# Loading the first two weight units in pieces, and moving two preparation steps behind the first tanh

## The chip, the cores and the metric

The kernel runs on one core of a Trainium2 chip. The metric is device time in microseconds (us) for one execution, on that core. Engines are named as the profile names them: PE (matrix products; PEld are its weight loads), DVE (vector engine), ACT (scalar engine), POOL (GpSimd) and SP (which issues most DMAs). Each engine takes its instructions in a fixed order and waits at each for what it needs.

## What is computed

Attention with two kinds of masks over 8 batches, 8 heads, 576 tokens and 64 dimensions, and then a gated feed-forward layer on the 4608 resulting rows of 512 numbers:

```
scores = q @ k.T / 8            # heads 0-3: the 32 keys up to the query; heads 4-7: every 4th key of 128
attn   = softmax(where(mask, scores, -1e9))
x      = (attn @ v), heads side by side          # (4608, 512)
g, val = x @ w_gate, x @ w_val                   # (4608, 1536)
out    = (g * sigmoid(g) * val) @ w_out          # (4608, 512)
```

All inputs and outputs are float32. To keep that precision, the kernel splits each number into a high half in fp32r, which PE multiplies fast, and the rest, the low half; a product is made as high x high, low x high and high x low.

## The kernel before

**Stages.** The rows of x are worked on as columns, in three chunks of 512 columns and then three pairs of chunks with a faster product scheme. The first chunk is the one that matters here. Its attention (four packs, m = 0 to 3) and the preparation of the first weights run together in the first 30 us, in an order that is written out by hand. After that, one **step** s handles 128 of the 1536 hidden columns: PE makes the gate product `bg` (12 matmuls of 128x512), the value product `bv` (12) and, for step s-1, the output product `bo` (12). Step 0 is made in two passes in `gv_first` (L590), as the halves of x come; the others by `gv_mm` (L578) and `out_mm` (L630). In steps 1 and 2 the eight products that need a high half of the weights come first and the four with the low half last.

**What one step does besides.** ACT takes the tanh of `bg` (L608); DVE multiplies it with `bg` (`dve_u`, L613), which also frees the bank of `bg` for the next step, and then with `bv` (`dve_h`, L618); ACT casts the result to its high half (`h_hi`, L623) and POOL subtracts to get the low half (`h_lo`, L628).

**Weight units.** The weights come from memory as 24 units of 128 x 768 numbers, two for each step (units 2s and 2s+1), each as 768 pairs of 32-bit words of a 64-bit number. A unit goes through five stages, named by the letters of `STAGES = "ETBHL"`:

- E, `w_exp` on ACT (L253): scales the upper words,
- T, `w_shift`: shifts the lower or the upper words, on ACT (L270) for units 0, 1, 3, 5, 6, 8, 9, 11, 13, ... and on DVE (L273) for units 2, 4, 7, 10, 12,
- B, `w_bits` on DVE: joins the two words into one float32 (L280 after an ACT shift, L283 after a DVE one), called the **joining** below,
- H, `w_split_hi` on ACT (L290): the **cast** to the high half,
- L, `w_split_lo` on POOL (L294): the subtraction that gives the **low half**.

Stages E and T work in the loaded buffer; B writes one of three buffers (chosen by the unit's number modulo 3, for units up to 19), so stage T or B of unit u must wait until the low half of unit u-3 has been taken. The stages of units 0 and 1 are cut into parts by `SPLIT = {0: (0, 2, 3), 1: (0, 1, 3)}` in thirds of a unit: the first part of unit 0 is two thirds, that of unit 1 one third, and these are all that step 0 needs. The rest of unit 1 (two thirds) goes into the first output product, `bo` of step 0.

**Loads.** `w_load` (L230) issues the DMA of the next unit on SP into one of six buffers, once the buffer's earlier unit has been joined. All loads of the first part go through SP's queue in the order of the code at L674 to L693: queries, keys and values of the four packs, unit 0 ahead of the values of packs 2 and 3, then unit 1, the rest of the masks, units 2 to 5 and the data of pack 4. SP keeps at most eight DMAs outstanding.

**What sets the order.** The first attention and units 0 to 3 follow the string at L708, word by word: Q, S, X, T, K, A, N, U are steps of the attention, H and L after it the split of x, Y and Z idle matmuls, `W`n the next whole stage n (numbers into "ETBHL"), `V`nup part p of stage n of unit u. What comes after (the loop at L992) is put in order by a scheduler, which picks by its own estimate of when each instruction is ready, with some orders held by `behind`. So a stage taken from the string may end up in another place against others on the same engine than the code suggests.

**The fifth pack.** Pack 4 belongs to the second chunk. Its scores are made on PE in step 2, and its `results` (L522) after step 4 or 5; these need `far_keys` (L511), a transpose on DVE.

## Time and profile before

| | before |
|---|---|
| median of 3 runs | 892.26 us (892.11 to 893.58) |
| the profiled execution | 890.97 us |
| its span, first to last instruction | 889.2 us |
| PE busy | 879.5 us, 99% of the span |
| DVE, ACT, POOL busy | 76%, 43%, 31% of the span |
| DMA | 207.91 MB, 234 GB/s on average; 343 and 379 GB/s in the first two of 40 slices |
| granted TensorE clock | full in all 40 slices |

The profiled execution is 1.77 us longer than its span, and 1.29 us below the median. PE is busy nearly all the time, so the shares of the other engines say little on the whole; the time that PE does not work lies in the first 30 us, and there the other engines count.

### The profile page before, as it was taken

Reading aid. Unit: us, or ns where it says so; the run is one execution under the profiler, and the core shown is the slowest. Engines: PE = TensorE matmul, PEld = TensorE weight load, DVE = VectorE, ACT = ScalarE, POOL = GpSimd, SP = SyncE. Lnnn points to the kernel's source line nnn. Section 1 sums busy time; section 2 is a strip of 40 time slices with the busy share of each in tenths; the row PEclk is TensorE's granted clock in tenths of the full one; section 3 lists DMA queues with packets and bytes.
Section 4 is the critical chain, followed back from the end, with each engine's and each line's share of the span. In section 5 each row is a group of like instructions: output and inputs, shape, how many; then the busy total and the mean of one; then the engine's idle time right before and its main releaser. Section 6 shows DMA issues by size and latency. Waiting matters only on the chain.

```text
span 889.2 us, 19625 instructions
## 1 busy us (share of the span) xinstructions
PE 879.5 (99%) x7954; PEld 719.1 (81%) x7954; DVE 675.8 (76%) x1067; ACT 380.4 (43%) x615; POOL 272.3 (31%) x313
## 2 busy tenths in 40 slices
PE   8999999999999999999999999999999999999998
PEld 5778888888888888888888888888888888888886
DVE  7876658997899993777699966787799755556963
ACT  6877533433332342333355533343455423334451
POOL 4967631211121222323333112333322113333310
PEclk9999999999999999999999999999999999999999
DMA  9975518768778775887777877887766776666672
GB/s 343 379 287 203 165 59 296 258 224 273 240 267 277 251 247 199 260 242 239 247 234 235 261 249 252 259 251 240 231 217 217 244 224 190 189 192 195 196 221 97
DMA packets 78698, 207.91 MB, mean 234 GB/s; under 512 B 9456, under 2 KB 28016, under 8 KB 78608
## 3 DMA queue, kind: packets, MB, share of 16 engines
q0 software_dynamic: 27520, 100.16, 36.8%
q1 hardware_dynamic: 41872, 70.33, 22.6%
q10 hardware_dynamic: 9216, 36.17, 11.7%
q8 instruction: 63, 1.03, 0.5%
q14 instruction: 27, 0.22, 0.1%
HBM read 159.96 MB, written 42.47 MB: 228 GB/s over the span
## 4 chain that ended last, share of the span: by engine, by line
PE 96%; DMA 2%; DVE 1%; ACT 0%; issue 0%; DVEq 0%; SPq 0%
PE bo L934 33%; PE bv L934 12%; PE bg L934 12%; PE bo L636 11%; PE bg L587 11%; PE bv L587 11%; PE two L522 3%; PE two L459 2%; DMA at_float<-qkb 1%; DMA at_int<-w 1%; ACT at_int L253 0%; DVE at_int L283 0%; DVE at_int L280 0%; DVE at_int L273 0%; ACT at_int L270 0%
## 5 line engine op out<-in xcount | busy, mean ns | idle before, releaser
L934 PE MATMUL bo<-at_float32r 128*128 128x512 f32 x1296 | 306.1, 390 | 0.0
L934 PEld LDWEIGHTS bo<-at_float32r 128*128 128x128 f32 x1296 | 242.5, 188 | 50.9
L861 POOL DMA_DIRECT2D at_float32r<-pieces x189 | 101.3, 536 | 351.0 <-PE bo L934 210.8
L895 DVE TENSOR_TENSOR at_float<-bo,at_float 128x512 f32<-128x512 f32 (+1 forms) x169 | 112.4, 679 | 66.7 <-PE bo L934 33.4
L895 DVE TENSOR_TENSOR at_float32r<-at_float,at_float32r 128x512 fp32r<-128x512 f32 (+1 forms) x147 | 112.2, 792 | 26.1 <-ACT at_float32r L924 19.5
L934 PE MATMUL bv<-at_float32r 128*128 128x512 f32 x486 | 128.2, 390 | 0.0
L934 PE MATMUL bg<-at_float32r 128*128 128x512 f32 x486 | 128.2, 390 | 0.0
L934 PEld LDWEIGHTS bg<-at_float32r 128*128 128x128 f32 x486 | 91.1, 188 | 19.0
L934 PEld LDWEIGHTS bv<-at_float32r 128*128 128x128 f32 x486 | 90.9, 188 | 19.1
L628 POOL TENSOR_TENSOR at_float32r<-at_float,at_float32r 128x512 fp32r<-128x512 f32 x36 | 51.5, 1431 | 172.8 <-PE bo L636 87.6
L636 PE MATMUL bo<-at_float32r,at_float32r 128*128 128x512 f32 x432 | 104.4, 390 | 0.0
L587 PE MATMUL bg<-at_float32r,at_float32r 128*128 128x512 f32 x420 | 101.9, 391 | 0.8 <-DVE at_float L613 0.8
L924 ACT CAST at_float32r<-at_float 128x512 fp32r<-128x512 f32 x126 | 75.4, 620 | 63.5 <-PE bv L934 16.3
L587 PE MATMUL bv<-at_float32r,at_float32r 128*128 128x512 f32 x420 | 101.7, 391 | 0.0
L636 PEld LDWEIGHTS bo<-at_float32r,at_float32r 128*128 128x128 f32 x432 | 80.7, 188 | 17.0
L587 PEld LDWEIGHTS bg<-at_float32r,at_float32r 128*128 128x128 f32 x420 | 78.3, 188 | 17.8 <-DVE at_float L613 1.2
L587 PEld LDWEIGHTS bv<-at_float32r,at_float32r 128*128 128x128 f32 x420 | 78.4, 188 | 16.6
L960 ACT ACTIVATE at_float<-at_float 128x512 f32<-128x512 f32 x72 | 45.4, 631 | 94.2 <-DVE at_float L895 94.2
L939 ACT COPY at_float<-bg 128x512 f32<-128x512 f32 x63 | 36.9, 586 | 87.8 <-PE bg L934 87.5
L895 POOL TENSOR_TENSOR at_float<-at_float,at_float 128x512 f32<-128x512 f32 x36 | 51.6, 1434 | 23.2 <-DVE at_float L963 13.0
L962 DVE SCALAR_TENSOR_TENSOR at_float<-at_float,at_float 128x512 f32<-128x512 f32 x72 | 49.4, 686 | 10.7 <-ACT at_float L960 10.1
L294 POOL TENSOR_TENSOR at_float32r<-at_int,at_float32r 128x768 fp32r<-128x768 f32 (+2 forms) x26 | 47.1, 1823 | 20.5 <-ACT at_float32r L290 20.5
(84 smaller groups left out, 856.3 us busy)
## 6 DMA issues: line engine op xcount, KB each, us to landing
at_float32r<-pieces POOLq DMA_DIRECT2D x189, 512.0 KB, 4.4
pieces<-at_float32r SPq DMA_DIRECT2D x126, 256.0 KB, 3.2
at_int<-w SPq DMA_DIRECT2D x24, 768.0 KB, 6.7
at_float<-vb ACTq DMA_DIRECT2D x31, 520.0 KB, 5.1
at_float<-qkb ACTq DMA_DIRECT2D x16, 640.0 KB, 6.6
out<-at_float SPq DMA_DIRECT2D x35, 256.0 KB, 4.0
at_float<-qkb ACTq DMA_DIRECT2D x15, 576.0 KB, 6.4
at_float<-at_float SPq DMA_DIRECT2D x128, 32.0 KB, 3.4
```

What stands on the lines that cost most here:

```text
L294: nc.gpsimd.tensor_tensor(out=lo, in0=wst[u]["y"][:, a:b].bitcast(F32), in1=hi, op=ALU.subtract)
L522: nc.tensor.matmul(out=two[BQ * j:BQ * j + BQ, p, (D + 1) * x:(D + 1) * (x + 1)], lhsT=t[r, BQ * i:BQ * i + BQ], rhs=v[r, i, :], start=Tru ...
L587: last["g", which] = nc.tensor.matmul(out=bank.rearrange("p (n c) -> p n c", n=2), lhsT=wcol(f, o, low), rhs=x[l][j], start=n == 0, stop=n ...
L628: last["l"] = nc.gpsimd.tensor_tensor(out=hl, in0=hst[i][0], in1=hst[i][1], op=ALU.subtract)
L636: nc.tensor.matmul(out=bank_o[j][:, :CH], lhsT=wcol(f, 2 * DM + P * j, low), rhs=x, start=f == 0 and low == 0 and x is hh, stop=f == NF - ...
L861: nc.gpsimd.dma_start(out=taken[asked], in_=pieces[asked % NPIECE])
L895: x = engine.tensor_tensor(out=out, in0=a, in1=b, op=op)
L924: nc.scalar.copy(out=o[:, 0], in_=src)
L934: nc.tensor.matmul(out=bank, lhsT=w, rhs=x, start=first and n == 0 and t in FRESH, stop=last and n == len(ops) - 1, skip_group_check=True)
L939: nc.scalar.copy(out=kept[KEPT[t]][r], in_=banks[0][r][:, :CS])
L960: nc.scalar.activation(out=f, in_=g, func=AF.Tanh, scale=0.5)
L962: nc.vector.scalar_tensor_tensor(out=f, in0=f, scalar=1.0, in1=g, op0=ALU.add, op1=ALU.mult)
```

## The change

Units 0 and 1 are loaded in two DMAs each. `w_load` takes only the first part of the cut (two thirds of unit 0, one third of unit 1); `w_rest` loads the rest. The rest of unit 0 is issued behind the values of pack 3, and the rest of unit 1 behind units 2 and 3, ahead of the masks. In the string, the scaling and the shift of unit 1 are done for its first third alone; the cast and the low half of unit 2 (`W3 W4`) and the joining of unit 3 (the last `W2`) are taken out. They come in the loop after the first tanh and `dve_u`, together with the scaling and shift of the rest of unit 1.

```
-            last["w"] = nc.sync.dma_start(out=t, in_=w[u // 2, u % 2].bitcast(I32))
+            now = slice(0, 2 * UT * SPLIT[u][1] if u in SPLIT else 2 * WU)
+            last["w"] = nc.sync.dma_start(out=t[:, now], in_=w[u // 2, u % 2].bitcast(I32)[:, now])
...
+    def w_rest(u):
+
+        o = 2 * UT * SPLIT[u][1]
+        last["w"] = nc.sync.dma_start(out=at(raw_at[u], 2 * WU, I32)[:, o:], in_=w[u // 2, u % 2].bitcast(I32)[:, o:])
...
         first_v(3, (act, act), sp)
+        w_rest(0)
         w_load()
+        w_load()
+        w_load()
+        w_rest(1)
         nc.sync.dma_start(out=consts[:, near:], in_=masks[:, near:])
...
-        for what in ("... V001 V101 Z2 A3 N2 U2 W0 "
-                     "Z3 H2 L2 W1 N3 V201 V301 V401 U3 W0 H3 L3 V210 V310 V410 W0 W1 W2 W1 W3 W4 W2").split():
+        for what in ("... V001 V101 Z2 A3 N2 U2 V010 "
+                     "Z3 H2 L2 V110 W0 N3 V201 V301 V401 U3 H3 L3 V210 V310 V410 W0 W1 W2 W1").split():
...
-        w_upto(L=W + 3, H=W + 4 - (s == 0))
+        if s > 0:
+            w_upto(L=W + 3, H=W + 4)
...
             if s == 0:
                 w_upto(T=4, B=4, H=4)
+                w_part("E", 1, 1)
+                w_part("T", 1, 1)
                 dve_h(0)
```

What this does to the order of instructions shows on POOL first. There, behind the first chunk's x, stand the low halves of units 2 and 3 (`128x768`), the low half of the rest of unit 1 (`128x512`, L294) and `h_lo` of step 0 (L628). Buffers `at_776` hold joined units (numbers 345, 409, 427 stand for units 0, 1, 2 and every third unit after). Before:

```order
L294 TENSOR_TENSOR at_1536_float32r<-at_776_int_427,at_1536_float32r 128x768
L294 TENSOR_TENSOR at_1536_float32r<-at_776_int_345,at_1536_float32r 128x768
L294 TENSOR_TENSOR at_1536_float32r<-at_776_int_409,at_1536_float32r 128x512
L628 TENSOR_TENSOR at_512_float32r<-at_512_float_216,at_512_float32r 128x512
L294 TENSOR_TENSOR at_1536_float32r<-at_776_int_409,at_1536_float32r 128x768
```

And now (lines L300 and L634 are L294 and L628 of before; the buffers are 347, 411, 429):

```order
L300 TENSOR_TENSOR at_1536_float32r<-at_776_int_429,at_1536_float32r 128x768
L300 TENSOR_TENSOR at_1536_float32r<-at_776_int_347,at_1536_float32r 128x768
L634 TENSOR_TENSOR at_512_float32r<-at_512_float_218,at_512_float32r 128x512
L300 TENSOR_TENSOR at_1536_float32r<-at_776_int_411,at_1536_float32r 128x512
L300 TENSOR_TENSOR at_1536_float32r<-at_776_int_411,at_1536_float32r 128x768
```

`h_lo` of step 0 now stands ahead of the low half of unit 1's rest.

On DVE, from the joining of unit 3 to the second `dve_h`: `bg` marks `dve_u` (L613), `bv` marks `dve_h` (L618), `128x3x256` are whole units and `128x2x256` the rest of unit 1. Before:

```order
L280 SCALAR_TENSOR_TENSOR at_776_int_345<-at_1536_int_185 128x3x256
L613 SCALAR_TENSOR_TENSOR at_512_float_216<-at_512_float_216,bg 128x512
L280 SCALAR_TENSOR_TENSOR at_776_int_409<-at_1536_int_180 128x2x256
L618 SCALAR_TENSOR_TENSOR at_512_float_216<-at_512_float_216,bv 128x512
L273 TENSOR_SCALAR at_776_int_409<-at_1536_int_187 128x3x256
L283 SCALAR_TENSOR_TENSOR at_776_int_409<-at_1536_int_187,at_776_int_409 128x3x256
L280 SCALAR_TENSOR_TENSOR at_776_int_427<-at_1536_int_189 128x3x256
L613 SCALAR_TENSOR_TENSOR at_512_float_239<-at_512_float_239,bg 128x512
L618 SCALAR_TENSOR_TENSOR at_512_float_239<-at_512_float_239,bv 128x512
```

And now:

```order
L619 SCALAR_TENSOR_TENSOR at_512_float_218<-at_512_float_218,bg 128x512
L286 SCALAR_TENSOR_TENSOR at_776_int_347<-at_1536_int_185 128x3x256
L624 SCALAR_TENSOR_TENSOR at_512_float_218<-at_512_float_218,bv 128x512
L286 SCALAR_TENSOR_TENSOR at_776_int_411<-at_1536_int_181 128x2x256
L279 TENSOR_SCALAR at_776_int_411<-at_1536_int_189 128x3x256
L619 SCALAR_TENSOR_TENSOR at_512_float_241<-at_512_float_241,bg 128x512
L289 SCALAR_TENSOR_TENSOR at_776_int_411<-at_1536_int_189,at_776_int_411 128x3x256
L624 SCALAR_TENSOR_TENSOR at_512_float_241<-at_512_float_241,bv 128x512
L286 SCALAR_TENSOR_TENSOR at_776_int_429<-at_1536_int_191 128x3x256
```

The first `dve_u` stands ahead of the joining of unit 3, and the second `dve_u` and `dve_h` stand between the stages of units 4 and 5.

Further on, on DVE, from the fifth `dve_u` to the first instruction that needs pack 4's results (`two`); the transpose (L511) is `far_keys` of pack 4. Before:

```order
L613 SCALAR_TENSOR_TENSOR at_512_float_216<-at_512_float_216,bg 128x512
L273 TENSOR_SCALAR at_776_int_345<-at_1536_int_168 128x3x256
L511 STREAM_TRANSPOSE at_512_float_349<-at_512_float_318 128x512
L283 SCALAR_TENSOR_TENSOR at_776_int_345<-at_1536_int_168,at_776_int_345 128x3x256
L618 SCALAR_TENSOR_TENSOR at_512_float_216<-at_512_float_216,bv 128x512
L280 SCALAR_TENSOR_TENSOR at_776_int_409<-at_1536_int_180 128x3x256
L530 TENSOR_SCALAR at_8_float_317<-two 128x8
```

And now:

```order
L619 SCALAR_TENSOR_TENSOR at_512_float_218<-at_512_float_218,bg 128x512
L279 TENSOR_SCALAR at_776_int_347<-at_1536_int_168 128x3x256
L289 SCALAR_TENSOR_TENSOR at_776_int_347<-at_1536_int_168,at_776_int_347 128x3x256
L624 SCALAR_TENSOR_TENSOR at_512_float_218<-at_512_float_218,bv 128x512
L286 SCALAR_TENSOR_TENSOR at_776_int_411<-at_1536_int_181 128x3x256
L517 STREAM_TRANSPOSE at_512_float_351<-at_512_float_320 128x512
L536 TENSOR_SCALAR at_8_float_319<-two 128x8
```

`far_keys` stands behind the joinings of units 12 and 13. On PE, the results of pack 4 and the scores of pack 5 stood between `bv` of step 4 and `bo` of step 3; now they stand behind that `bo`. The two mask products of pack 4's scores stood in the middle of step 0's second pass and now stand behind it. On ACT the first tanh stands ahead of the cast of unit 2 instead of behind it, and the third to fifth tanh have more casts, scalings and shifts of units ahead of them. From step 6 on, the order on all engines is the same.

## Rows read from the trace of the kernel before

**Rows 1.** Busy time by stretch: length, PE, PEld, DVE, ACT, POOL, clock, DMA, GB/s.

```profile
20.00:30.00 10.00, 8.46 (x64) 5.72 (x64) 9.78 (x14) 9.42 (x16) 9.57 (x8) 1.00 1.02 413
30.00:60.00 30.00, 30.00 (x193) 24.60 (x192) 20.74 (x24) 24.58 (x35) 24.46 (x15) 1.00 0.88 318
```

**Rows 2.** PE's waits from 30 us to the end: total, times, longest.

```profile
PE bg L587 <- DVE at_float L613: 0.8, 1, 0.8
```

**Rows 3.** Timeline of PE: start us, us, engine, line, instruction, [idle before, releaser].

```profile
26.38 1.09 PE L596 MATMUL bg<-at_float32r,at_float32r 128*128 128x512 f32 x4
...
28.14 0.73 PE L596 MATMUL bv<-at_float32r,at_float32r 128*128 128x512 f32 x2 [0.21 <-POOL at_float32r L294]
29.62 3.02 PE L587 MATMUL bg<-at_float32r,at_float32r 128*128 128x512 f32 x12 [0.76 <-DVE at_float L613]
...
61.18 0.79 PE L522 MATMUL two<-at_float,at_float 64*32 64x65 f32 x60 [0.29 <-issue]
```

**Rows 4.** Chain that ended last, in time: start us, us, what.

```profile
35.36 2.72 PE bo L636 x12
38.08 2.72 PE bg L587 x12
...
55.45 2.72 PE bg L587 x12
...
62.65 2.95 PE bo L636 x12
65.60 2.72 PE bg L587 x12
```

**Rows 5.** Timeline of ACT.

```profile
21.45 0.92 ACT L253 ACTIVATE at_int<-at_int 128x768 f32<-128x768 f32 x1 [0.29 <-DMA at_int<-w]
...
27.52 0.83 ACT L290 CAST at_float32r<-at_int 128x768 fp32r<-128x768 f32 x1 [0.17 <-DVE at_int L283]
28.26 0.59 ACT L608 ACTIVATE at_float<-bg 128x512 f32<-128x512 f32 x1
...
43.17 0.84 ACT L290 CAST at_float32r<-at_int 128x768 fp32r<-128x768 f32 x1 [0.65 <-DVE at_int L283]
...
51.13 0.58 ACT L608 ACTIVATE at_float<-bg 128x512 f32<-128x512 f32 x1
```

**Rows 6.** Timeline of DVE.

```profile
27.43 1.47 DVE L280 SCALAR_TENSOR_TENSOR at_int<-at_int 128x768 int32<-128x768 int32 x1
28.88 0.69 DVE L613 SCALAR_TENSOR_TENSOR at_float<-at_float,bg 128x512 f32<-128x512 f32 x1
...
33.87 0.95 DVE L273 TENSOR_SCALAR at_int<-at_int 128x768 int32<-128x768 int32 x1 [2.21 <-POOL at_float32r L294]
...
39.28 1.87 DVE L280 SCALAR_TENSOR_TENSOR at_int<-at_int 128x768 int32<-128x768 int32 x1 [1.11 <-ACT at_int L270]
...
42.05 1.09 DVE L283 SCALAR_TENSOR_TENSOR at_int<-at_int,at_int 128x768 int32<-128x768 int32 x1
...
58.91 0.69 DVE L613 SCALAR_TENSOR_TENSOR at_float<-at_float,bg 128x512 f32<-128x512 f32 x1 [3.16 <-ACT at_float L608]
...
60.38 0.70 DVE L511 STREAM_TRANSPOSE at_float<-at_float 128x512 f32<-128x512 f32 x1
...
63.30 0.16 DVE L530 TENSOR_SCALAR at_float<-two 128x8 f32<-128x8 f32 x1
```

**Rows 7.** Line L280, the joinings after an ACT shift: duration ns min/median/max.

```profile
L280 DVE SCALAR_TENSOR_TENSOR at_int<-at_int x16: 458/950/1867, 18.5 to 108.9; 128x768 int32<-128x768 int32 x12, 128x512 int32<-128x512 int32 x2, 128x256 int32<-128x256 int32 x2
```

**Rows 8.** Timeline of POOL.

```profile
26.63 1.45 POOL L294 TENSOR_TENSOR at_float32r<-at_int,at_float32r 128x256 fp32r<-128x256 f32 x1
28.43 5.40 POOL L294 TENSOR_TENSOR at_float32r<-at_int,at_float32r 128x768 fp32r<-128x768 f32 x3 [0.35 <-ACT at_float32r L290]
33.80 1.29 POOL L628 TENSOR_TENSOR at_float32r<-at_float,at_float32r 128x512 fp32r<-128x512 f32 x1
36.86 3.47 POOL L294 TENSOR_TENSOR at_float32r<-at_int,at_float32r 128x768 fp32r<-128x768 f32 x2 [1.77 <-ACT at_float32r L290]
```

More of the change, by code (lines that the diff above doesn't have):

```diff
@@ L707, in attention_moe @@
     with tc.manual_schedule(engines={et.PE, et.DVE, et.Activation, et.Pool}):
-        for what in ("Q0 S0 Q1 Y2 S1 X0 Q2 X1 T0 S2 T1 K0 K1 Q3 X2 A0 T2 K2 S3 X3 N0 A1 V000 U0 T3 V100 K3 N1 A2 V200 U1 H0 L0 V300 V400 H1 L1 V001 V101 Z2 A3 N2 U2 W0 "
-                     "Z3 H2 L2 W1 N3 V201 V301 V401 U3 W0 H3 L3 V210 V310 V410 W0 W1 W2 W1 W3 W4 W2").split():
+        for what in ("Q0 S0 Q1 Y2 S1 X0 Q2 X1 T0 S2 T1 K0 K1 Q3 X2 A0 T2 K2 S3 X3 N0 A1 V000 U0 T3 V100 K3 N1 A2 V200 U1 H0 L0 V300 V400 H1 L1 V001 V101 Z2 A3 N2 U2 V010 "
+                     "Z3 H2 L2 V110 W0 N3 V201 V301 V401 U3 H3 L3 V210 V310 V410 W0 W1 W2 W1").split():
             first[what[0]](*[int(c) for c in what[1:]])
```

## The prediction

> **What bounds the kernel now.** The busy shares come first and say where not to look: PE works 99% of the span. PE's waits from 30 us to the end are then one wait of 0.8 us for `dve_u` [rows 2], and in the timeline a gap of 0.29 us ahead of pack 4's results [rows 3]; behind these PE has no slack anywhere. Two things follow. A microsecond that PE starts step 1 earlier can only be kept if nothing else makes PE wait later, and a microsecond of new waiting in the first steps stays until the end. The chain that ended last shows the same: from step 1 on it is PE's groups end to end, a dozen products in 2.72 us, that is 0.227 us each [rows 4]. Then the stretches. From 20 to 30 us ACT, DVE and POOL are busy 9.4 to 9.8 of 10 us; from 30 to 60 us they are busy 20.7 to 24.6 of 30 us, with the clock at full speed throughout [rows 1]. So between the start and the first output rows the three helpers have some 5 to 9 us of slack, and the question is at which instructions it lies.
>
> At the start, PE's first pass over `bg` ends at 26.38 + 1.09 = 27.47 [rows 3], but the first tanh starts at 28.26, behind the cast of unit 2 [rows 5]; `dve_u` then starts at 28.88, with the joining of unit 3 ahead of it until 28.90 [rows 6], and PE starts step 1 at 29.62 [rows 3]. That is the wait of 0.8 us.
>
> **The loads.** Between 20 and 30 us 413 GB/s arrive [rows 1]. Unit 1 was scaled from 21.45 on, after ACT had waited 0.29 us for it [rows 5], so it had landed by 21.43. A third of a unit is 256 KB, or 0.63 us at that rate. By my count of what now stands ahead of each load (an estimate from that rate), unit 2 has landed by 22.1, the rest of unit 1 by 25.2, and unit 4 near 27.5 as before. The rest of unit 1 is first touched by ACT behind the cast of unit 2, near 28.9, so 3.7 us of other work hide it. What the pieces give is the 0.29 us of waiting and two thirds of two ACT instructions of 0.92 us, 1.2 us, ahead of the first tanh [rows 5]; but the first tanh waits for PE's pass anyway, so I put this at nothing, at best 0.3 us.
>
> **The start of step 1: a gain.** With the cast moved behind it the first tanh runs at 27.5 to 28.1 (0.59), `dve_u` at 28.13 to 28.82 (0.69) [rows 5, 6]. PE's own pass still ends with the pair at 28.14 + 0.73 = 28.87 [rows 3], and the two mask products, now behind it (half of 0.227 us each), end with it or 0.1 us later. Step 1 starts at 28.95 in place of 29.62: **-0.65 us**.
>
> **POOL: the gain is lost.** The cast of unit 2 now runs at 28.05 to 28.9, so POOL starts on its low half at 28.95 where it did at 28.43. Before, three subtractions (units 2, 3 and the rest of unit 1) took 5.40 us, to 33.83, and `h_lo` came fourth, 1.29 us [rows 8]. Now `h_lo` comes third, and the rest of unit 1 ends at 28.95 + 5.40 + 1.29 = 35.64. Bounds: without any hold-up two units take 3.47 us [rows 8] and the two of 512 columns 1.29 us each, 35.0 in all; with one hold-up more, 36.2. I take 35.64, because the joinings of unit 3 and of the rest of unit 1 still fall beside these subtractions, as they did within the 5.40.
>
> What such a hold-up is, the rows show: a joining begun beside a subtraction takes 1.47 or 1.87 us in place of 0.95 [rows 6, 7], and both ended 0.82 us after the subtraction did (28.90 against 26.63 + 1.45 = 28.08, and 41.15 against 36.86 + 3.47 = 40.33) [rows 6, 8]. A joining that starts second waits for the end of the subtraction, and the reverse gives POOL its 5.40 for 4.76 of work.
>
> The Trainium skill ("SBUF — State Buffer", section "SBUF: two separate sides") has this as an exclusive lock: of a DVE instruction with two SBUF inputs and a GpSimd one, whichever starts first keeps the port for its whole length. By that rule alone, with DVE first at each meeting, POOL would end at the later bound, and the sum would be that of the heavier rival below; with POOL first it would end near 35.0. The 0.82 us agree with it; who comes first in the new order no run shows yet.
>
> Who waits for the 35.64? First PE. Step 1's `bg` takes 3.02 us and `bv` 2.72 [rows 3, 4], so the first output product runs at 34.69 to 34.92; the second needs the low half of unit 1's rest and waits 0.7 us. `bo` ends at 38.15 in place of 38.08: the 0.65 us are gone. Second, DVE: the shift of unit 4 uses that unit's buffer. Before, it waited 2.21 us for the same subtraction and started at 33.87 [rows 6]; now it starts at 35.65. Queued behind it on DVE are `dve_u` of step 1, the joining of unit 4, `dve_h` and the joining of unit 5, 1.8 us later than before, and PE's step 2 needs both `dve_u` and unit 4.
>
> **Step 2: a new wait of PE.** The shift ends at 36.6 (0.95), `dve_u` at 37.25 (0.69), the joining at 38.2 (0.95), the cast at 39.05 (0.84) [rows 5 to 7]. The `bg` of step 2 starts at 39.1 and not at 38.08, and takes 3.02 us, as the one behind a wait did, and not 2.72: +1.3 us. Its last four products need the low half of unit 4, which POOL has at 39.1 + 1.74 = 40.84 (half of 3.47) or, held up by the joining of unit 5, up to 0.95 later, while PE is there at 41.2: 0 to 0.6, I take 0.3. Sum from here: **+1.6 us**; the `bg` of step 4 starts at 55.45 + 1.6 = 57.05.
>
> **The units behind it, and pack 4.** `dve_h` of step 1 ends at 38.85, the joining of unit 5 at 39.8, its cast at 40.65. On ACT now come `h_hi` (as the tanh, 0.59), the scaling and the shift of unit 6 (0.92 each); each starts some 0.1 us before the end of the one ahead (28.26 against 27.52 + 0.83 = 28.35) [rows 5], so the shift ends at 42.9 and the joining of unit 6 starts at 42.95, where it was 39.28 [rows 6]: +3.7 us, twice what PE lost. From there to the end of the joining of unit 7 were 39.28 to 43.14, 3.86 us [rows 6], and now a `dve_u` (0.69) stands between: 47.5. From the cast of unit 7 to the end of the fourth tanh ACT took 43.17 to 51.71, 8.54 us, for ten other instructions [rows 5]; they are the same in another order, so that tanh ends at 56.0. It does not stop PE: `dve_u` ends at 56.75, 0.3 us before step 4 wants it. But behind it on DVE are a shift, `dve_h` and the joinings of units 10 and 11 (four of 0.68 to 0.95, the last beside a subtraction): unit 11 is joined at 61.1, cast by ACT at 62.0, and the fifth tanh, behind that cast now, ends at 62.6. Then DVE has the same six instructions as before from `dve_u` on, 58.91 to 63.30, 4.39 us [rows 6], with `far_keys` last and not third. They end at 67.0; with two joinings of six beside subtractions (0 to 0.9 each) I take 67.3.
>
> PE comes to pack 4's results after `bv` of step 4 and `bo` of step 3, 57.05 + 8.16 = 65.2, and stands there 2.1 us, where before it stood 0.29 for a transpose that ended at 61.08 [rows 3, 6]. Results and scores take 61.18 to 62.65, 1.47 us [rows 3, 4], and the group behind them 0.23 us more than 2.72 (2.95) [rows 4]. The `bg` of step 5 starts at 67.35 + 1.47 + 0.23 = 69.05 in place of 65.60 [rows 4]: **+3.45 us**. From step 6 on the orders are equal, and PE has nothing in which to make it up [rows 2].
>
> The profiled execution was 890.97 us, its span 1.77 us less; 890.97 + 3.45 = 894.4. The median of the runs is 1.29 us above the profiled one: 895.7.
>
> **Rivals.** *Heavier:* the joinings win the race against the subtractions, and on the way from the low half of unit 1's rest to `far_keys` four meetings (units 5, 7, 11 and 12) cost 0.4 us more each, half of the 0.82 that a meeting costs the later one. +1.6: 897.3. For it: the 5.40 for 4.76, three subtractions that lost 0.6 already. Against it: my sum has two of them in.
>
> *On the other side, not slower:* the slack of the helpers takes up the delay of 3.7 us before pack 4 asks for it. For it: 5 to 9 us of slack from 30 to 60 us [rows 1]. Its point: `far_keys` done by 65.2. Then PE has the wait of step 2 alone, +1.6: 893.9, or 893.0 where POOL has no hold-up and step 2 starts at 38.4. Against it: ACT's order is fixed, and what is idle in it stands ahead of casts that now come later still.
>
> *The change does what it says and nothing else:* the rest of unit 1 is in time, PE keeps its 0.65: 891.6. It needs the low half by 34.9, before POOL's lower bound, so it has little for it. That the pieces do not land as planned would show as a wait for a load; with 3.7 us of margin I give that nothing.
>
> **How the numbers follow.** About 0.2%, 1.8 us, is what a measurement of this kernel can tell from no change: slower begins at 894.04, faster below 890.48. My forecast, about 895.7 with 894.5 to 896.5 by its own bounds, has 0.66; the heavier case 0.17; the slack case 0.14; the kept gain 0.03. So slower 0.82, the same 0.16 and faster 0.02. The range goes from 893.4, in the middle of the slack case, to 898.0, the heavier one with 36.2 for POOL's bound.
>
> **What would show it.** Right: the first tanh near 27.5 and step 1 near 28.95; the rest of unit 1 subtracted by 35.6 on POOL, with PE waiting within the first `bo`; a wait of about 1 us at the second `bg` for a cast; the joining of unit 6 near 43; PE waiting about 2 us ahead of pack 4's results for the transpose, which ends near 67. Wrong: no wait at the results (then +1.6 at most), or waits of PE in steps 6 and later, which would mean that the delay of the units outlives pack 4 and the loss is larger.

## The result and the profile after

| | before | after |
|---|---|---|
| median, 6 runs each | 892.39 us (892.11 to 894.59) | 898.64 us (898.32 to 899.86) |
| the profiled execution | 890.97 us | 898.32 us |
| its span | 889.2 us | 896.2 us |

The change makes the kernel slower: the medians differ by 6.25 us, and the ratio estimated from all runs is 1.0066, with a 95% interval of 1.0053 to 1.0079. The forecast was +3.4 us, 895.7 us, with a range up to 898.0: the direction was right and the size too small. Lines from L246 on have moved by six in the changed kernel (L587 is now L593, L613 L619, L290 L296, L294 L300, L511 L517, L522 L528).

PE's waits from 30 us to the end, where before had one [rows 2]; columns are total, times, longest:

```profile
PE two L528 <- DVE at_float L517: 2.2, 1, 2.2
PE bg L593 <- DVE at_float L619: 0.6, 1, 0.6
PE bg L593 <- ACT at_float32r L296: 0.5, 1, 0.5
PE bo L642 <- POOL at_float32r L300: 0.4, 1, 0.4
PE bg L593 <- POOL at_float32r L300: 0.3, 1, 0.3
```

The wait of 0.8 us for the first `dve_u` is gone, and five others have come. Their places are in the timeline of PE, to be read against [rows 3, 4]:

```profile
25.86 1.23 PE L602 MATMUL bg<-at_float32r,at_float32r 128*128 128x512 f32 x4
...
28.59 2.06 PE L593 MATMUL bg<-at_float32r,at_float32r 128*128 128x512 f32 x8
30.99 1.21 PE L593 MATMUL bg<-at_float32r,at_float32r 128*128 128x512 f32 x4 [0.34 <-POOL at_float32r L300]
...
35.56 2.83 PE L642 MATMUL bo<-at_float32r,at_float32r 128*128 128x512 f32 x11 [0.38 <-POOL at_float32r L300]
38.87 3.42 PE L593 MATMUL bg<-at_float32r,at_float32r 128*128 128x512 f32 x12 [0.48 <-ACT at_float32r L296]
...
57.54 3.03 PE L593 MATMUL bg<-at_float32r,at_float32r 128*128 128x512 f32 x12 [0.60 <-DVE at_float L619]
...
68.23 0.81 PE L528 MATMUL two<-at_float,at_float 64*32 64x65 f32 x60 [2.21 <-DVE at_float L517]
...
69.73 4.49 PE L593 MATMUL bg<-at_float32r,at_float32r 128*128 128x512 f32 x12
```

Step 1 starts at 28.59. POOL's low half holds PE in `bg` of step 1 and in `bo` of step 0, a cast holds step 2, `dve_u` holds step 4, and the results of pack 4 wait 2.21 us for `far_keys`. The last line is the surprise: the `bg` of step 5 takes 4.49 us. In this view a dozen products take 2.88 us behind another group, 3.02 or 3.03 behind a wait or the small products, and 3.42 at step 2. The 3.42 hold a second wait, which shows at the weight loads: those of the last four products wait for the low half of unit 4.

```profile
41.08 0.77 PEld L593 LDWEIGHTS bg<-at_float32r,at_float32r 128*128 128x128 f32 x4 [0.54 <-POOL at_float32r L300]
```

The stretches around step 5 (length, PE, PEld, DVE, ACT, POOL, granted clock, DMA share, GB/s) say why its `bg` is slow:

```profile
66.00:69.80 3.80, 1.59 (x130) 1.41 (x129) 2.17 (x4) 2.19 (x3) 2.77 (x2) 0.96 0.67 210
69.80:74.20 4.40, 4.40 (x14) 3.51 (x14) 3.66 (x7) 0.00 (x0) 2.27 (x2) 0.65 0.92 363
74.20:77.00 2.80, 2.80 (x14) 2.30 (x13) 2.08 (x3) 2.75 (x5) 0.00 (x0) 1.00 0.36 149
```

Behind the wait the granted clock is 0.65 on average for 4.4 us, then full again; from 70 to 72 us it is 0.50, that is 1.2 GHz, half of the upper level of 2.4. In time at the lower level that is 4.4 x 0.35 / 0.5 = 3.1 us, and 3.8 x 0.04 / 0.5 = 0.3 us ahead of it: 3.4 us, which cost half of that, 1.7.

**Counted from one point.** The attention ahead of step 0 ends at another time in every execution: the first pass over `bg` ended between 26.86 and 28.03 us in the fifteen traces of the experiments. (It ended at 27.35 on average in the fourteen traces with loads in pieces, and at 27.78 in the three without, that of before among them. That may be the gain of the pieces that the forecast put at nothing; three traces are too few to show it.) So the starts of the later groups are best counted from there (27.47 before, 25.86 + 1.23 = 27.09 after), by the timeline's starts in both:

| start of `bg` of step | before | after | later by | as forecast |
|---|---|---|---|---|
| 1 | 2.15 | 1.50 | -0.65 | -0.65 |
| 2 | 10.45 | 11.78 | 1.33 | 1.2 |
| 3 | 19.49 | 21.39 | 1.90 | 1.6 |
| 4 | 27.82 | 30.45 | 2.63 | 1.6 |
| 5 | 37.97 | 42.64 | 4.67 | 3.45 |
| 6 | 46.13 | 52.41 | 6.28 | 3.45 |
| 7 | 55.92 | 62.25 | 6.33 | 3.45 |

The forecast read its starts from the chain [rows 4], where a group starts when the one before it ends. In the timeline a group that follows without a wait starts 0.16 us earlier (37.92 and not 38.08), so for step 2, which waits, the last column has 39.1 - 37.92.

The 6.33 us of the traces agree with the 6.25 of the medians. From there on both kernels do the same. The stretch from the `bg` of step 8 to the end took 797.3 to 798.7 us in all traces but that of e15 (804.0), without relation to the edits, so that nothing is read from differences under 1 us in a single trace's span.

POOL and DVE at the start of step 1, to be read against [rows 6, 8]. POOL:

```profile
28.52 4.58 POOL L300 TENSOR_TENSOR at_float32r<-at_int,at_float32r 128x768 fp32r<-128x768 f32 x2 [0.80 <-ACT at_float32r L296]
33.06 1.29 POOL L634 TENSOR_TENSOR at_float32r<-at_float,at_float32r 128x512 fp32r<-128x512 f32 x1
34.31 1.19 POOL L300 TENSOR_TENSOR at_float32r<-at_int,at_float32r 128x512 fp32r<-128x512 f32 x1
...
51.92 1.75 POOL L300 TENSOR_TENSOR at_float32r<-at_int,at_float32r 128x768 fp32r<-128x768 f32 x1
...
61.80 3.47 POOL L300 TENSOR_TENSOR at_float32r<-at_int,at_float32r 128x768 fp32r<-128x768 f32 x2
```

DVE:

```profile
28.36 0.95 DVE L286 SCALAR_TENSOR_TENSOR at_int<-at_int 128x768 int32<-128x768 int32 x1
...
35.54 0.95 DVE L279 TENSOR_SCALAR at_int<-at_int 128x768 int32<-128x768 int32 x1 [4.05 <-POOL at_float32r L300]
...
42.44 1.13 DVE L286 SCALAR_TENSOR_TENSOR at_int<-at_int 128x768 int32<-128x768 int32 x1 [3.02 <-ACT at_int L276]
...
52.15 2.07 DVE L486 TENSOR_TENSOR at_float<-at_float,at_float 128x512 f32<-128x512 f32 x1
...
63.66 2.42 DVE L289 SCALAR_TENSOR_TENSOR at_int<-at_int,at_int 128x768 int32<-128x768 int32 x1
...
67.47 0.70 DVE L517 STREAM_TRANSPOSE at_float<-at_float 128x512 f32<-128x512 f32 x1
```

The low half of unit 1's rest ends at 35.50, which is 8.41 us after the first pass (35.64 and 8.17 were forecast). The shift of unit 4 starts at 35.54 after 4.05 us of idle time, the joining of unit 6 at 42.44, and `far_keys` ends at 68.17. On ACT:

```profile
47.29 0.83 ACT L296 CAST at_float32r<-at_int 128x768 fp32r<-128x768 f32 x1 [2.82 <-DVE at_int L289]
...
54.25 0.63 ACT L498 ACTIVATE at_float<-at_float 128x512 f32<-128x512 f32 x1 [0.89 <-DVE at_float L486]
...
54.92 0.63 ACT L493 ACTIVATE at_float<-at_float 128x512 f32<-128x512 f32 x1
...
56.18 0.59 ACT L614 ACTIVATE at_float<-bg 128x512 f32<-128x512 f32 x1
```

From the cast of unit 7 to the end of the fourth tanh it is 47.29 to 56.77, 9.48 us. L498 and L493 are the two exponentials of pack 4.

### The profile page after: what moved, and what is told of

Read it like the earlier page. It is cut to its first block, busy times and chain, and to the rows that moved or that the text cites. A ratio compares the mean times of both kernels' runs of the same rounds, so it can differ in the third digit from the quotient of the medians.

```text
span 896.2 us, 19629 instructions
## 1 busy us (share of the span) xinstructions
PE 883.7 (99%) x7954; PEld 719.8 (80%) x7954; DVE 676.7 (76%) x1067; ACT 380.4 (42%) x617; POOL 272.8 (30%) x313
## 3 DMA queue, kind: packets, MB, share of 16 engines
q8 instruction: 63, 1.03, 0.5%
## 4 chain that ended last, share of the span: by engine, by line
PE 92%; DVE 1%; DMA 1%; ACT 0%; issue 0%; DVEq 0%
PE bo L944 33%; PE bv L944 12%; PE bg L944 12%; PE bo L642 10%; PE bg L593 10%; PE bv L593 10%; PE two L528 3%; PE two L465 2%; DMA at_int<-w 1%; DVE at_int L286 0%; DVE at_float L486 0%; ACT at_int L259 0%; ACT at_int L276 0%; DVE at_float L485 0%; DVE at_float L624 0%
## 5 line engine op out<-in xcount | busy, mean ns | idle before, releaser
L593 PE MATMUL bg<-at_float32r,at_float32r 128*128 128x512 f32 x420 | 104.4, 397 | 1.5 <-DVE at_float L619 0.6
L634 POOL TENSOR_TENSOR at_float32r<-at_float,at_float32r 128x512 fp32r<-128x512 f32 x36 | 52.3, 1453 | 174.6 <-PE bo L642 94.2
L593 PE MATMUL bv<-at_float32r,at_float32r 128*128 128x512 f32 x420 | 102.0, 392 | 0.0
L593 PEld LDWEIGHTS bg<-at_float32r,at_float32r 128*128 128x128 f32 x420 | 79.0, 190 | 20.4 <-POOL at_float32r L300 1.3
L593 PEld LDWEIGHTS bv<-at_float32r,at_float32r 128*128 128x128 f32 x420 | 78.4, 188 | 16.9
L300 POOL TENSOR_TENSOR at_float32r<-at_int,at_float32r 128x768 fp32r<-128x768 f32 (+2 forms) x26 | 46.6, 1802 | 26.1 <-ACT at_float32r L296 26.1
```

The costliest lines, as they stand in the source:

```text
L300: nc.gpsimd.tensor_tensor(out=lo, in0=wst[u]["y"][:, a:b].bitcast(F32), in1=hi, op=ALU.subtract)
L593: last["g", which] = nc.tensor.matmul(out=bank.rearrange("p (n c) -> p n c", n=2), lhsT=wcol(f, o, low), rhs=x[l][j], start=n == 0, stop=n ...
L634: last["l"] = nc.gpsimd.tensor_tensor(out=hl, in0=hst[i][0], in1=hst[i][1], op=ALU.subtract)
```

## The experiments

Every time is given against the kernel before, measured beside it on the same chip (on the chips used, its median was 891.35 to 892.45 us). The edits are against the changed kernel unless a line says otherwise, and e1 to e15 are numbered in the order in which they ran. The absolute times in the expectations are on the scale of the first measurement (892.39 before, 898.64 changed), so they are compared by their distance from the kernel before.

### Is it the clock, or something else at step 5

Two kernels give PE idle products in the place of the wait at the results. In both, a trace line tells more than the time does.

```diff
-        visits(m, a, a + 4)
+        visits(m, a + (m == 5), a + 4)
...
+        if s == 4:
+            with behind("o"):          # the last product of bo
+                idle(10, bank_g)
         attend(3 * s + 2)              # now holds pack 4's results
```

**e1, idle.** Expected:

> The changed kernel with ten idle products (bf16, 512 columns, into the bank of bg, which is free there) between bo of step 3 and pack 4's results, so that PE works through the 2.21 us in which it waited for far_keys; all other orders are unchanged. Theory A: the changed kernel's loss is 4.20 us of waiting up to the bg of step 5 and 1.70 us more because the clock was granted at 1.2 GHz behind that wait; with PE at work the results still start near 68.2, but the bg of step 5 takes 2.7 to 3.0 us in place of 4.42, and the time falls by 1.4 to 1.7 us, to about 897.1. Rival B: that group is slow for another reason (363 GB/s of DMA in this stretch, or the small products ahead of it), it stays at about 4.4 us, and the time stays at 898.6.

Measured: 897.34 us, 5.99 us above before (ratio 1.0065, interval 1.005 to 1.008), where the changed kernel was 6.25 above. PE's timeline:

```profile
66.03 2.33 PE L673 MATMUL bg<-at_float 128*128 128x512 bf16 x10
...
69.78 3.02 PE L593 MATMUL bg<-at_float32r,at_float32r 128*128 128x512 f32 x12
...
85.02 0.50 PE L642 MATMUL bo<-at_float32r,at_float32r 128*128 128x512 f32 x1
86.75 2.77 PE L642 MATMUL bo<-at_float32r,at_float32r 128*128 128x512 f32 x11 [1.23 <-issue]
```

With PE at work the group takes 3.02 us and not 4.49, at the same start of 69.8: the rival that something else slows it falls. The time, though, fell by 0.26 us only, where theory A said 1.4 to 1.7: 1.23 us are lost again within `bo` of step 5, with no releaser that the profile names. Counted from the first pass, the `bg` of step 6 starts 1.59 us earlier than in the changed kernel, and that of step 7 only 0.15.

```diff
+                for _ in range(2):
+                    nc.tensor.matmul(out=bank_g[:64]..., lhsT=ones, rhs=ones...)   # float32, 512 columns
+                idle(2, bank_g)
```

**e5, idle wide.** Expected:

> As the run with ten idle products, but with four that take as long (two in float32, four passes each, and two in bf16), so that PE's stream grows by six instructions and not by twenty. In the run before, bg of step 5 took 2.95 us at full clock, and then PE stood 1.23 us ahead of the second product of bo of step 5, with no engine named as releaser. Theory A: that new stall belongs to the longer stream of PE instructions; here it is gone or smaller, and the time is 4.5 to 4.9 us above the kernel before. Rival B: it belongs to the preparation, which is not ready earlier than in the changed kernel, whatever PE does in between; it stays at 1.2 us, and the time is 6.0 us above the kernel before.

Measured: 896.91 us, 5.47 us above before (1.0067, 1.005 to 1.0084).

```profile
85.75 1.43 PE L642 MATMUL bo<-at_float32r,at_float32r 128*128 128x512 f32 x5
87.52 1.89 PE L642 MATMUL bo<-at_float32r,at_float32r 128*128 128x512 f32 x7 [0.34 <-issue]
```

The new stall is 0.34 us and stands behind the fifth product instead of the first. The page counts 20 more PE and PEld instructions than in the changed kernel in the first of these and 12 in the second: eight fewer, four products with their weight loads, which is by how much the stall has moved. So it sits at one instruction of PE's stream, and it ends 1.73 and 1.77 us after PE has started the first product behind the small ones of pack 5 (at 85.02 and 85.75). Its cause is not shown; that PE's instructions arrive late there fits, and in the changed kernel PE would reach that instruction (the twelfth product) later than this. The time was between the two theories because of it, 0.6 us above what theory A gave.

Whether the clock falls is also a matter of the single execution. Seven traces of this document have a wait of more than 2 us at a pack's results and no idle products. Behind it the clock fell in three (the changed kernel, 2.21 us; e3, 2.23; e15, 2.97) and stayed full in four (e6, 2.46 us; e7, 2.52; e14, 2.99; e9, 3.55). So the full clock of e1 and e5 does not show that the idle products kept it up. In e6 and e9, without them, the `bg` of step 5 took 2.91 and 3.01 us at a full clock, and so it is the clock that makes the 4.49. The times point the same way: in the runs of e3 below the execution with a mean clock of 1.0 took 894.65 us and the three with 0.998 took 896.07 to 896.89; in e7 it is 895.57 and 895.78 against 897.00 and 898.60. But a mean does not say where the clock fell: the trace of e8, with 0.998, has its fall between 4 and 12 us and a full clock from there on, and its 892.61 us lie among the other runs of e8. And one run of the changed kernel does not fit: it had a mean of 1.0 and took 898.34 us, no less than the others.

### Which orders make far_keys late

```diff
-            w_upto(E=W + 6, T=W + 5, B=W + 5)
+            w_upto(E=W + 6, T=W + 5)
+            with behind(*["k"] * (s == 4)):     # k: far_keys
+                w_upto(B=W + 5)
...           # dve_h(4) and the next joining likewise
```

**e2, far keys.** Expected:

> The changed kernel with far_keys of pack 4 back at its old place on DVE: the joinings of units 12 and 13 and dve_h of step 4 are held behind it. Theory A: far_keys ends near 64.4, PE reaches the results at 66.0 and does not wait for them, the clock stays full, and bg of step 5 starts near 67.7, 2.1 us later than before (what step 2 and step 4 had lost): about 894.8, from 894.3 to 895.3. Rival B: the joinings that now come later make PE wait in step 5 or 6 for 1 us or more: 896 or above.

Measured: 893.80 us, 2.45 us above (1.0026, 1.0015 to 1.0037). PE waits 0.2 us for `far_keys`, the `bg` of step 5 takes 3.01 us, the clock stays full:

```profile
64.08 0.70 DVE L517 STREAM_TRANSPOSE at_float<-at_float 128x512 f32<-128x512 f32 x1
```

```profile
67.89 3.01 PE L593 MATMUL bg<-at_float32r,at_float32r 128*128 128x512 f32 x12
```

One instruction three places further up on DVE is worth 3.8 us, as theory A had it: some 2.0 of waiting and some 1.6 of clock.

```diff
                 w_part("L", 1, 1)
-                h_lo(0)
+                with behind("y"):               # y: the last low half
+                    h_lo(0)
```

**e3, pool order.** Expected:

> The changed kernel with one exchange on POOL: the low half of the rest of unit 1 ahead of h_lo of step 0, as before. Theory A: that low half ends near 34.3 and not 35.5, the shift of unit 4 starts 1.2 us earlier, and with it all that hangs on it up to far_keys: PE waits little in bo of step 0, bg of step 2 starts near 37.7, the wait at the results stays near 2.2 us with the clock's fall behind it. The time falls by 1.2 us to 897.4. Rival B: far_keys does not hang on unit 4 but on the order of ACT's instructions; then only step 2 comes earlier, the wait at the results grows by as much, and the time stays at 898.6.

Measured: 896.14 us, 4.79 us above (1.005, 1.0035 to 1.0065), 1.46 less than the changed kernel. The `bg` of step 2 starts 10.55 us after the first pass and not 11.78; the wait at the results is 2.2 us as in the changed kernel, with a granted clock of 0.72 behind it:

```profile
67.43 0.88 PE L528 MATMUL two<-at_float,at_float 64*32 64x65 f32 x60 [2.23 <-DVE at_float L517]
...
69.18 4.06 PE L593 MATMUL bg<-at_float32r,at_float32r 128*128 128x512 f32 x12
```

`far_keys` ends 39.86 us after the first pass, 1.22 earlier than in the changed kernel. So the chain up to `far_keys` hangs on the shift of unit 4, and that on POOL's order, as theory A had it.

**e4, both.** Expected:

> The edits of the two runs before together (low half of unit 1's rest ahead of h_lo, and far_keys at its old place). Theory A: the two gains are of different waits and add up: 894.8 less 1.2, about 893.6, with step 2 near 37.7 and no wait at the results. Rival B: one wait behind the other takes the second gain: 894.8.

Measured with both edits: 892.11 us, 0.76 us above (1.0009, 0.9999 to 1.0018). The gains add up (3.8 and 1.46 of 6.25 leave 1.0). In steps 1 to 5 two waits of PE are left, 0.32 us in the `bg` of step 1 and 0.60 at that of step 4.

### Which part of the change

```diff
 # e6: the string of the changed kernel, with the three steps back at its end
-... U3 H3 L3 V210 V310 V410 W0 W1 W2 W1"
+... U3 H3 L3 V210 V310 V410 W0 W1 W2 W1 W3 W4 W2"
 # e7: the kernel before, without them there
-... V410 W0 W1 W2 W1 W3 W4 W2"
+... V410 W0 W1 W2 W1"
```

**e6, parts.** Expected:

> The first part of the change alone: units 0 and 1 loaded in pieces, the scaling and shift of the rest of unit 1 behind the first dve_u; the cast and low half of unit 2 and the joining of unit 3 stay ahead of the first tanh. h_lo of step 0 stands ahead of the low half of unit 1's rest here too, and far_keys behind the joinings of units 12 and 13. Theory A: the loss comes from that order and from the two added ACT instructions, not from the three moved steps; step 1 starts near 29.5 as before, and the time is 5 to 7 us above the kernel before. Rival B: the three moved steps cost the time; this is within 1 us of the kernel before.

Measured: 897.04 us, 5.60 us above (1.0061, 1.0046 to 1.0076). Step 1 starts 2.17 us after the first pass, as before; PE waits 1.3 us for `dve_u` at step 4 and 2.46 us at the results.

**e7, tail.** Expected:

> The second part of the change alone: cast and low half of unit 2 and joining of unit 3 behind the first tanh and dve_u; loads, scaling and shift of unit 1 whole and in their old places. h_lo of step 0 stands ahead of the low half of unit 1's rest, and far_keys behind the joining of unit 12. Theory A: step 1 starts near 28.6 as in the changed kernel; the shift of unit 4 starts near 35.3 all the same, since POOL's order is the cause; ACT is 1.3 us freer in steps 0 and 1, so the later waits are smaller: 2 to 4 us above the kernel before. Rival B: the two added ACT instructions are the cause; then this keeps its earlier start: 0.5 to 1 us below the kernel before.

Measured: 896.39 us, 4.95 us above (1.0059, 1.0044 to 1.0074), more than the 2 to 4 expected. Step 1 starts 1.51 us after the first pass. There is no wait at step 4, and 2.52 us at the results, with `far_keys` behind one joining more than before. Either part alone is enough: in both, `h_lo` stands ahead of the low half on POOL and `far_keys` later on DVE, and the costs of the two do not add up.

```diff
 # e8: e7 with the edits of e2 and e3; e12: e6 with the edits of e2 and e3
```

**e8, tail ordered.** Expected:

> The second part of the change alone, with the low half of unit 1's rest held ahead of h_lo of step 0 and the joinings of units 12 and 13 held behind far_keys, as in the kernel before. Theory A: the earlier start of step 1 (28.6 in place of 29.62) is kept, as nothing behind it is later: 0.6 to 1.0 us below the kernel before. Rival B: the preparation of units 2 and 3, 0.1 to 0.5 us later on POOL, takes it all: no difference.

Measured: 892.47 us, 1.03 us above (1.001, 1.0001 to 1.0019). Here the expected gain did not come. Step 1 starts 1.50 us after the first pass, 0.65 earlier than before, but PE then waits 0.31 us for unit 2's low half and 0.29 us for `dve_u`, and loses some 0.1 us more in the products behind each wait: step 2 starts at 10.85, 0.40 later than before. The earlier start is eaten within one step.

**e12, parts ordered.** Expected:

> The first part of the change alone (loads in pieces, scaling and shift of unit 1's rest behind the first dve_u), with the low half of unit 1's rest ahead of h_lo and far_keys at its old place. Theory A: what is left is the two added ACT instructions, which make the fourth tanh late; PE waits 0.6 to 1.3 us at step 4 and nowhere else: 0.8 to 1.6 us above the kernel before. Rival B: with the old orders ACT has room for them: within 0.4 us of the kernel before.

Measured: 893.07 us, 1.25 us above (1.0016, 1.0007 to 1.0025), as theory A had it. Nearly the whole loss is this line of PE:

```profile
57.06 3.06 PE L593 MATMUL bg<-at_float32r,at_float32r 128*128 128x512 f32 x12 [1.32 <-DVE at_float L619]
```

So the wait at step 4 comes with the first part of the change, not from POOL's order: it is there in every kernel that has this part with pack 4's exponentials in their place, and not in e7 and e8. What that part adds on ACT is two instructions (0.70 and 0.69 us in the changed kernel); that they and not the cut loads are the cause was not tested apart.

### The wait at step 4, and the port

```diff
 # visits: pack 4's scores, shift and exponentials one place later, behind bg of step 3
-        visits(m, a, a + 4)
+        visits(m, a + (m == 4), a + 4)
```

**e9, early tanh.** Expected:

> The changed kernel with pack 4's scores one place later, behind bg of step 3, so that its two exponentials stand behind the fourth tanh on ACT and not ahead of it. In the changed kernel that tanh runs at 56.18, 5 us after its bg, and PE waits 0.60 us for the dve_u behind it at step 4. Theory A: this wait goes (bg of step 4 starts 0.7 us earlier), but far_keys hangs on the joinings of units 12 and 13 and not on PE, so that the wait at the results grows by what was saved: 5.5 to 6.3 us above the kernel before. Rival B: the two waits are independent, and 0.7 us are saved: 5.3 us or less above it.

Measured: 898.90 us, 7.08 us above (1.0082, 1.0067 to 1.0098): worse than theory A said. The wait at step 4 is gone, and the one at the results is

```profile
68.53 0.81 PE L528 MATMUL two<-at_float,at_float 64*32 64x65 f32 x60 [3.55 <-DVE at_float L517]
```

1.3 us longer and not 0.7. The profiled execution, with a full clock, took 895.71 us; the other three, with means of 0.996 to 0.998, 898.5 to 899.4.

**e10, three orders.** Expected:

> Low half of unit 1's rest ahead of h_lo, far_keys at its old place, and pack 4's scores behind bg of step 3, all together. The first two alone gave 0.76 us above the kernel before, with a wait of 0.6 us left at step 4. Theory A: that wait goes too, and as far_keys is not the last thing in this kernel nothing takes its place: 0.0 us, between 0.3 below and 0.3 above the kernel before. Rival B: the later exponentials make far_keys late again: 0.8 us above or more.

Measured with the edits of e2, e3 and e9: 892.15 us, 0.33 us above (1.0006, 0.9997 to 1.0014). The wait at step 4 is gone, but 1.09 us at the results have come: the two theories each hold in part. Counted from the first pass, the `bg` of step 8 starts 1.50 us later in this trace than in that of before, so the two measures differ by over 1 us here. By the medians it is no slower than before, as far as they can tell, and no faster.

```diff
-                w_upto(T=4, B=4, H=4)
+                w_upto(T=4, H=3)
...
                 dve_h(0)
+                with behind("h"):
+                    w_upto(B=4, H=4)             # on top of e2 and e3
```

**e11, joining later.** Expected:

> Low half of unit 1's rest ahead of h_lo and far_keys at its old place, as in the run that gave 0.76 us above the kernel before, and the joining of unit 3 behind dve_h of step 0 instead of ahead of it. In the changed kernel this joining starts 0.16 us before POOL's subtraction of unit 2 and runs its full speed (0.95 us), while the two subtractions of units 2 and 3 take 4.58 us for 3.47. Theory A: whoever starts first goes first; now the subtraction does, it ends near 30.3, the wait of 0.34 us within bg of step 1 goes, and the joining takes 1.2 us or more. Unit 3 is then later by 1 us, and with it POOL's next subtractions and the shift of unit 4: 0.8 to 1.4 us above the kernel before. Rival B: the two share the port, the subtraction is as slow as before, and the wait within bg stays 0.3 us.

Measured: 892.67 us, 0.85 us above (1.001, 1.0001 to 1.0019). POOL and DVE:

```profile
28.39 1.76 POOL L300 TENSOR_TENSOR at_float32r<-at_int,at_float32r 128x768 fp32r<-128x768 f32 x1 [0.80 <-ACT at_float32r L296]
```

```profile
29.02 1.95 DVE L286 SCALAR_TENSOR_TENSOR at_int<-at_int 128x768 int32<-128x768 int32 x1
```

The subtraction that starts first takes its full speed, 1.76 us, and the wait in `bg` of step 1 is gone. The joining begun beside it ends at 30.97, 0.82 us after the subtraction (30.15), as in the two cases before the change [rows 6, 8]. In the changed kernel it was the other way: the joining started first (28.36, 0.95 us), and the two subtractions took 4.58 us for 3.47, the first of them 2.42. The Trainium skill ("SBUF — State Buffer", section "SBUF: two separate sides") says that whichever of the two starts first keeps the shared port for the whole instruction; both traces agree, with these numbers.

### Taking the results out of the way

```diff
-        visits(m, a, a + 4)
+        visits(m, a + 2 * (m == 5), a + 4)      # pack 4's results behind bg of step 5
```

**e13, results later.** Expected:

> The changed kernel with pack 4's results (and pack 5's scores) behind bg of step 5 instead of ahead of it; no instruction is added, and the orders up to step 4 are unchanged. Theory A: PE finds bg of step 5 ready at 66.0, the results at 68.7 find far_keys done at 68.2, and no clock falls; what is left is what steps 2 and 4 lost, 2.6 us by bg of step 4: 2.3 to 3.0 us above the kernel before, as with far_keys at its old place. Rival B: the preparation of units 10 to 13 is late by as much as far_keys, and PE waits for it in step 5 instead: 4.5 us above or more.

Measured: 895.24 us, 3.52 us above (1.0039, 1.0025 to 1.0053). PE finds pack 4's results ready, the clock stays full, and the `bg` of step 6, with the same work ahead of it as before, starts 48.59 us after the first pass and not 46.13: 2.5 us lost, as in e2. But 1.52 us of waiting have come at pack 5's results, since its scores are issued with pack 4's results. Neither theory holds: the wait is new, as in B, but it is for the pack and not for units.

**e14, four orders.** Expected:

> The kernel with three restored orders (0.33 us above the kernel before, with a wait of 1.09 us left at pack 4's results), and pack 4's results behind bg of step 5. Theory A: the wait goes and nothing takes its place: 0.5 to 1.2 us below the kernel before. Rival B: the norm and shift of packs 4 and 5, now later on DVE, make PE wait at another place: 0.3 us above or more.

Measured with the edits of e2, e3, e9 and e13: 895.50 us, 3.78 us above (1.0043, 1.0029 to 1.0056). The one long wait:

```profile
83.05 0.80 PE L528 MATMUL two<-at_float,at_float 64*32 64x65 f32 x60 [2.99 <-ACT at_int L276]
```

The profile puts it down to a shift on ACT; pack 5's `far_keys` ended 0.1 us ahead of it (82.23 + 0.71 = 82.94), and that is what the results need. So rival B holds: the wait has moved to another place.

**e15, packs later.** Expected:

> The kernel of e14 with the results of packs 5 and 6 moved along as well (pack 5's by two places, pack 6's by one). Theory A: the preparation of the weights is in time once POOL's and DVE's orders are restored, and the waits at the results were the packs' own; none is left, and the start of step 1 is kept: 0.3 to 1.0 us below the kernel before. Rival B: a wait of 1 us or more shows at another step, because the units are still late: 0.8 us above or more.

Measured: 898.40 us, 5.95 us above (1.0062, 1.0049 to 1.0076). Up to step 8, whose `bg` starts 64.86 us after the first pass (64.08 before), PE waits for weights once, 0.33 us for a low half in step 1. Then it waits 0.6 us for `dve_h` and 3.0 us at the results of pack 6, and behind these the clock falls (0.50 from 102 to 104 us). Rival B's wait is there, but for the pack and not for units. A pack needs some 12 to 15 us from the end of its scores to the end of `far_keys` (14.1 for pack 4 before, 12.5 and 14.4 for pack 5 in e13 and e14, 15.0 for pack 6 in e15), and a place that is moved for one moves the next. No version was found that beats the kernel before.

## Why the prediction was right or wrong

**Right.** Step 1 starts 0.65 us earlier, to the hundredth. POOL's order is what loses it: the low half of unit 1's rest ended 8.41 us after the first pass (8.17 forecast), and e3, which exchanges two instructions there, takes 1.46 us off. The step from there to unit 4 and to the `bg` of step 2 (11.78 after the first pass; 39.1 - 27.47 = 11.6 forecast), the added 0.57 us between steps 2 and 3 (0.4 forecast by the same starts, 0.3 of it for unit 4's low half), and the wait at the results (2.21; 2.1 forecast) are all in the trace with about these sizes, and e2 and e3 show the two causes apart. Two sizes are right by luck. In step 1 the forecast had one wait of 0.7 us in `bo`; the trace has 0.34 us in `bg`, where the forecast had none, and 0.38 in `bo`. And the wait at the results kept its length because PE and `far_keys` were both later than forecast. Loads cost nothing, as forecast: PE's waits name none.

**Wrong: the sum has no term for the clock.** The step "PE ... stands there 2.1 us" took the wait at its own length. The `bg` behind it took 4.49 us, and the delay grew by 6.28 - 4.67 = 1.61 us. What slows the group is the clock: at a full one, from the same start, it took 3.02 us in e1. What makes the clock fall in one execution and not in another stays open, as four traces kept it through waits as long. What the fall costs in the end was not told apart so well: the executions of e3 and e7 with a lower and a full mean clock differ by 1.2 to 3.0 us, the idle products gave back only 0.26 and 0.78 us, a stall at a fixed instruction taking part of it. The 1.61 us are over half of the error of 2.8 us; without them the time would be near 897.0, inside the range.

**Wrong: "It does not stop PE".** The fourth tanh was to end at 56.0 and `dve_u` 0.3 us before PE wants it; the sum put no wait at step 4. There was one of 0.60 us, and 0.73 us went there (2.63 - 1.90). The term that failed is ACT's 8.54 us for "the same in another order", which became 9.48. They are not the same: before, one of pack 4's two exponentials stood ahead of that tanh and the other behind it, and now both stand ahead. The first of them also waited 0.89 us for a DVE instruction (L486) that started 0.23 us behind a subtraction and took 2.07 us, ending 0.55 us after it. Before it took 0.92:

```profile
49.64 0.92 DVE L480 TENSOR_TENSOR at_float<-at_float,at_float 128x512 f32<-128x512 f32 x1
```

The hold-ups were counted for the joinings alone; this instruction reads two operands too. That the first part of the change brings this wait is shown by e12 against e8, and that the place of the exponentials decides it by e9; what the two added ACT instructions do in it was not taken apart further.

**Wrong in size: the hold-ups.** The joining of unit 3 won the race for the port, so that the two subtractions took 4.58 us (3.47 without a hold-up) and step 2 came 0.15 us later than forecast, relative to the first pass; and the joining of unit 12 took 2.42 us, so that `far_keys` ended 1.3 us later than forecast, relative to the first pass. That one instruction accounts for it: the fifth tanh ahead of it ended no later than forecast. As PE was later too by then, the wait at the results was hardly longer than forecast. The heavier rival had this mechanism, and its 897.3 without the clock is near the 4.67 us that were lost by step 5, 1.2 more than forecast.

**The rival "slack"** had no part in it: `far_keys` was 2.2 us late. The part of the rival "kept gain" that a good order can show was tried in e8: the earlier start is lost within step 1 even then, to two waits of 0.3 us. The first of them stands in the changed kernel too (0.34 us), and the forecast did not have it.

## What to carry to other kernels

Before moving a step behind another, look at which engine's order it changes besides its own: here two neighbours exchanged on POOL and one transpose three places later on DVE made most of the loss, while the step itself gained what was counted. Where a forecast makes TensorE wait 2 us where it waited none, add a term for the clock behind the wait, with a chance and not as a certainty (1.6 us in the changed kernel; the clock fell in three traces of seven). And an engine with slack on average (5 of 30 us on ACT) had none at the one tanh that PE was to wait for.

## What the runs showed of the hardware

- A wait of PE of 2.21 us was followed by 3.4 us at half clock in the changed kernel (granted clock 0.65 over 4.4 us), and waits of 2.23 and 2.97 us by a fall in e3 and e15, but not in every execution: the profiled ones of e6, e7, e14 and e9 show a full clock behind waits of 2.46, 2.52, 2.99 and 3.55 us.
- PE's stream has a place where it stood with no releaser: 1.23 us with 20 added instructions ahead of it (e1), 0.34 us with 12 (e5), at the same instruction, each ending about 1.75 us after the start of the first product behind 256 small products and weight loads. The cause stays open.
- A wait of PE costs a little more than its length: a group of twelve products took 3.02 us behind a wait of 0.76 us before the change, 3.03 behind one of 0.60 after it, and 2.88 behind another group.
- Of a DVE instruction with two operands and a POOL subtraction that meet, the one that starts second pays: the joining ended 0.82 us after the subtraction in e11, and in the changed kernel the subtraction that started 0.16 us behind the joining took 2.42 us, where it took 1.76 in e11.
